# wo brought block by block, its first block on partitions 0 to 63 by eight transfers of eight partitions

## Chip, cores and metric

The kernel runs on one core of one Trainium2 chip. The metric is the device time of one execution in microseconds (us). Clock times below are us from the start of the profiled execution.

## The reference, cut to what matters

A decode step: attention for 4 tokens with 32 heads over an 8192-entry K and V cache (512 MB), the output projection with `wo` (4096 x 1024, 8 MB), and beside it a small MLP. The two results are mixed by a sigmoid gate.

```python
q = (x @ wq).reshape(B, Sq, H, Dh)
scores = einsum("bhqd,bhkd->bhqk", q, k_cache) * Dh ** -0.5
o = einsum("bhqk,bhkd->bhqd", softmax(scores), v_cache)
a = o.reshape(B, Sq, H * Dh) @ wo          # the part that the change touches
out = g * a + (1 - g) * b                  # b: the MLP branch
```

## The kernel before

K and V come in 64 pieces of 4 MB each, through a ring of five buffers. V lags K by four steps. At the end the projection multiplies the attention rows `LT` by `wo`, in eight blocks of 512 rows (1 MB, 8 KB on each of the 128 partitions, as the rows of the on-chip memory are called; 8 matmuls). The last group of heads must be finished (`flush`, `o_rows`) before the last two blocks can be used; blocks 0 to 5 need only what is known before the loop ends.

```python
ring = ctx.enter_context(tc.tile_pool(name="ring", bufs=5))
def slot():
    return ring.tile([P, RING], BF, name="piece", tag="piece")    # 128 x 32 KB
wov = A_wo.rearrange("(g p r) n -> p g r n", p=P, r=FR)           # FR = 4, 8 blocks g
# ... cut ...
def wo_piece(g0, g1, r0=0, r1=FR):
    ng, nr = g1 - g0, r1 - r0
    w = slot()[:, :ng * nr * D].rearrange("p (g r n) -> p g r n", g=ng, r=nr)
    nc.sync.dma_start(out=w.rearrange("p g r n -> p g (r n)"),
                      in_=wov[:, g0:g1, r0:r1].rearrange("p g r n -> p g (r n)"))
    def use():
        for g in range(ng):
            for r in range(nr):
                for n in range(NH):
                    mm_acc(acc[:, n * NB:(n + 1) * NB], LT[:, r0 + r, g0 + g, :], w[:, g, r, n * NB:(n + 1) * NB])
    return use
# ... cut ...
for u in range(NT + LAG):                 # NT = 64, LAG = 4
    if u < NT:
        k_piece(u)
    if u >= LAG:
        v_piece(u - LAG)                  # the last V piece comes in four transfers of 1 MB
    # ... cut: side work early in the loop ...
    if u == NT:
        o_rows(0, GE)                     # GE = 6: LT of blocks 0 to 5
        add_x()
GS = NWB // 2
last = [wo_piece(0, GS), wo_piece(GS, GE), wo_piece(GE, NWB - 1),
        wo_piece(NWB - 1, NWB, 0, FR - 1), wo_piece(NWB - 1, NWB, FR - 1, FR)]
flush()
o_rows(GE, NWB)
for use in last:
    use()
```

Of the kernel before, what the change touches and what calls it, by code (L numbers as in the profile page):

```python
# [9 lines left out]
BF = mybir.dt.bfloat16  # L10
F32 = mybir.dt.float32
# [8 lines left out]
def kernel(  # L20
# [22 lines left out]
    nc = tc.nc  # L43
    P = 128
    Bn, Sq, D = A_x.shape
# [11 lines left out]
    NT = Bn * H // HT  # L57
    LAG = 4
    FR = 4
    FG = F // (P * FR)  # L60
    NB = 512
    NH = D // NB
# [7 lines left out]
    const = ctx.enter_context(tc.tile_pool(name="const", bufs=1))  # L70
# [7 lines left out]
    ops = ctx.enter_context(tc.tile_pool(name="ops", bufs=2, space=PSUM))  # L78
    o2p = ctx.enter_context(tc.tile_pool(name="o2p", bufs=1, space=PSUM))

    def slot():
        return ring.tile([P, RING], BF, name="piece", tag="piece")
# [13 lines left out]
    identb = const.tile([P, P], BF)  # L96
# [37 lines left out]
    qa = const.tile([P, 4, H, Bn], BF)  # L134
    OT = const.tile([P, H, Bn], BF)
    LT = const.tile([P, FR, H // FR, Bn], BF)
    hT = const.tile([P, FG, FR, Bn], BF)
    sgb = const.tile([P, 2, Bn], F32)
    c12 = const.tile([P, 2, Bn], F32)
# [7 lines left out]
    acc = accp.tile([Bn, D], F32)  # L147

    def mm_acc(out_ap, lhsT, rhs, start=False):
        nc.tensor.matmul(out_ap, lhsT=lhsT, rhs=rhs, start=start, stop=True, skip_group_check=True)  # L150
# [15 lines left out]
    def add_x():  # L166
        xb = ptp.tile([Bn, D], BF, name="xb", bufs=1)
        nc.sync.dma_start(out=xb[:], in_=x2)
        xf = ptp.tile([Bn, D], F32, name="xf", bufs=1)
        nc.vector.tensor_copy(out=xf[:], in_=xb[:])  # L170
        for n in range(NH):
            mm_acc(acc[:, n * NB:(n + 1) * NB], dg[:], xf[:, n * NB:(n + 1) * NB])
# [50 lines left out]
    WB = P * FR // Dh  # L223
    NWB = H // WB

    def o_rows(g0, g1):

        n = g1 - g0
        lp = ops.tile([P, FR, n, Bn], F32, name="o_ps")
        for k in range(WB):  # L230
            for r in range(FR):
                nc.tensor.matmul(lp[32 * k:32 * k + 32, r], lhsT=identb[:, r:P:FR],
                                 rhs=OT[:, WB * g0 + k:WB * g1:WB, :], start=True, stop=True, skip_group_check=True)
        nc.vector.tensor_copy(out=LT[:, :, g0:g1, :], in_=lp[:])

    def wo_piece(g0, g1, r0=0, r1=FR):
        ng, nr = g1 - g0, r1 - r0
# [10 lines that stand above are left out]
# [6 lines left out]
    def flush():  # L254
        while pending:
            pending.pop(0)()
# [8 lines left out]
    def k_piece(u):  # L265
        b, h0 = heads(u)
        g, t = divmod(u, GT)
        Z = Zt[u % 2]
        for a in range(NQ):
            nc.gpsimd.tensor_copy(out=Z[32 * a:32 * a + 32, :, 31 + 32 * a:32 + 32 * a],  # L270
                                  in_=qa[32 * a:32 * a + 32, :, h0 + a // QH, b:b + 1])
        if t == 0:
            S_ps[g] = scp.tile([P, 512], F32, name="S_ps")
        sps = S_ps[g]
        kn = slot()
        nc.sync.dma_start(out=kn[:], in_=kv_view(A_k_cache, u))
        for c in range(JR // CJ):
            T = ttp.tile([P, CJ, 2, 32, 2], BF, name="T", tag="T")
            nc.vector.transpose(out=T[:].rearrange("p j h i e -> p (j h i e)").bitcast(U32),  # L279
                                in_=kn[:, c * CJ * Dh:(c + 1) * CJ * Dh].bitcast(U32))  # L280
            for jl in range(CJ // 16):
                jc = c * (CJ // 16) + jl
                s = 31 - (JC * t + jc)
                for he in range(4):
                    half, e = divmod(he, 2)
                    nc.tensor.matmul(sps[:, :], lhsT=Z[:, he, s:s + P], rhs=T[:, 16 * jl:16 * jl + 16, half, :, e],  # L286
                                     start=(t == 0 and jc == 0 and he == 0),
                                     stop=(t == GT - 1 and jc == JC - 1 and he == 3))
            if c == 0:
                flush()  # L290
        if t == GT - 1:
            softmax(g)
# [34 lines left out]
    def v_piece(u):  # L327
        b, h0 = heads(u)
        g, t = divmod(u, GT)
        B_ = PB[g % 2]  # L330
        vn = slot()
        vv = kv_view(A_v_cache, u)
        cut = 4 if u == NT - 1 else 1
        for c in range(cut):
            lo, hi = c * RING // cut, (c + 1) * RING // cut
            nc.sync.dma_start(out=vn[:, lo:hi], in_=vv[:, lo:hi])
        o_ps = ops.tile([P, 4 * Dh], F32, name="o_ps")
        n = 0
        for jc in range(JC):
            for uq in range(4):  # L340
                j0 = 16 * jc + 4 * uq
                nc.tensor.matmul(o_ps[32 * t:32 * t + NM, :], lhsT=B_[:, JC * t + jc, uq].rearrange("p s j -> p (s j)"),  # L342
                                 rhs=vn[:, j0 * Dh:(j0 + 4) * Dh], start=(n == 0), stop=(n == JR // 4 - 1))
                n += 1
                if n == 8:
                    flush()
        o_sb = OS[g % 2]
        nc.scalar.copy(out=o_sb[32 * t:32 * t + NM, :], in_=o_ps[32 * t:32 * t + NM, :])  # L348
        if t < GT - 1:
            return  # L350

        def finish():
            oT = o2p.tile([P, GH], F32, name="oT")
            for q in range(4):
                nc.tensor.matmul(oT[:, :], lhsT=o_sb[:, q * Dh:(q + 1) * Dh],  # L355
                                 rhs=selg[:, q].rearrange("p t s -> p (t s)"), start=(q == 0), stop=(q == 3))
            hg = h0 + HT - GH
            nc.vector.scalar_tensor_tensor(out=OT[:, hg:hg + GH, b], in0=oT[:, :], scalar=sgb[:, 1, b:b + 1],  # L358
                                           in1=rinv_t.pop(g)[:], op0=ALU.mult, op1=ALU.mult)
        pending.append(finish)  # L360
# [8 lines left out]
    GE = NWB - GH // WB  # L369
    for u in range(NT + LAG):  # L370
# [3 lines that stand above are left out]
            v_piece(u - LAG)  # L374
        if side:
            side.pop(0)()
        if u == NT:
            o_rows(0, GE)
            add_x()
    GS = NWB // 2  # L380
    last = [wo_piece(0, GS), wo_piece(GS, GE), wo_piece(GE, NWB - 1),
            wo_piece(NWB - 1, NWB, 0, FR - 1), wo_piece(NWB - 1, NWB, FR - 1, FR)]
    flush()
    o_rows(GE, NWB)
    for use in last:
        use()
# [35 lines left out]
```

## Time and profile before

| | before |
|---|---|
| median time (4 runs beside the change) | 1355.85 us |
| span of the profiled execution | 1354.6 us |
| last V piece landed | 1325.4 us |
| first wo transfer (4 MB) landed | 1335.38 us |
| last wo transfer landed | 1345.35 us |
| last matmul ended | 1351.7 us |

Two lines of the page: the busy share of the 16 DMA engines in 40 slices of the span, in tenths, and the DMA queue that carries the data (packets, MB, share of 16 engines' span).

```profile
DMA  9999999999999999999999999999999999999996
q1 hardware_dynamic: 21904, 575.69, 99.0%
```

So the kernel is a stream of bytes until its last 20 us or so. The end of the chain of waits (start, duration, what) shows what those are. PE is TensorE, `o_ps` the attention weights times V, `acc` the sum of the projection.

```profile
1287.47 7.01 PE o_ps L342 x32
...
1295.99 39.39 DMA piece<-in_A_wo_dram
1335.38 0.04 issue
1335.42 16.27 PE acc L150 x64
1351.69 0.02 issue
1351.71 0.57 ACT res L390
```

The 39.39 us are one wo transfer from issue to landing: it stands in line behind V, whose last landing is at 1325.4. After it come all 64 matmuls of the projection in one go. The first transfer holds four blocks, so nothing can start before all 4 MB are there. The same in stretches (from:to, length, busy time and count on PE, PE's weight loads, VectorE, ScalarE and GpSimd, then granted TensorE clock, DMA share, GB/s):

```profile
1315.00:1318.00 3.00, 3.00 (x17) 1.22 (x15) 0.00 (x0) 0.58 (x1) 0.00 (x0) 1.00 1.00 418
...
1330.00:1340.00 10.00, 5.51 (x33) 2.21 (x33) 0.43 (x2) 0.00 (x0) 0.00 (x0) 0.66 0.92 381
1340.00:1346.00 6.00, 6.00 (x29) 2.39 (x28) 0.00 (x0) 0.00 (x0) 0.00 (x0) 0.99 0.41 165
1346.00:1355.00 9.00, 5.68 (x27) 2.04 (x24) 0.68 (x1) 0.57 (x1) 0.00 (x0) 0.93 0.00 1
```

TensorE is half idle while the last bytes come (1330 to 1340, at a clock of 0.66: the clock records put it at half from 1333.25 to 1340.07, beginning in an idle stretch of 4.16 us), and busy for 5.68 us when no byte is left to come. The DMA share falls to 0.41 in 1340 to 1346. The reason is in the landings. In the trace a piece of V raises its completion semaphore, the counter that tells of its landing, 16 times, which I read as once for each of the 16 engines. For the wo transfer of 0.75 MB these times, read from the trace's semaphore events, are:

```
1336.63 1336.76 1336.98 1337.96 1338.01 1339.47 1339.65 | 1343.22 | 1344.25 1344.26 1344.28 1344.36 1344.36 1344.60 1344.63 1344.71
```

Seven engines are ahead of the other nine, by 3.6 us and more (1339.65 against 1343.22).

### The profile page before, as it was taken

The page shows a single profiled execution, that of the slowest core. Times are in us where ns is not written, and L with a number is a line of the kernel's source. Part 1 is how long each engine was busy: PE and PEld are TensorE (multiplying, and loading weights), DVE is VectorE, ACT ScalarE, POOL GpSimd, SP SyncE. Part 2 cuts the span into 40 slices and gives each one's busy share as a digit, 9 for nine tenths or more (in the row PEclk, how much of TensorE's full clock was granted, in tenths as well). Part 3 has the DMA queues.
Part 4 walks back from the last instruction along what each step waited for, and adds up shares of the span by engine and source line. Part 5 has one row for each costly group of instructions (what it writes and reads, how often), then busy time and mean ns, then how long its engine had stood idle before and what let it go on. Part 6 is the DMA issues. An engine that isn't in the chain of part 4 may idle for free.

```text
span 1354.6 us, 11809 instructions
## 1 busy us (share of the span) xinstructions
PE 1065.1 (79%) x5112; PEld 434.5 (32%) x5112; DVE 622.3 (46%) x403; ACT 71.0 (5%) x118; POOL 86.8 (6%) x326
## 2 busy tenths in 40 slices
PE   2775888888687878879787777868877787888797
PEld 2432333333233323333233333323333332333333
DVE  1553345544543554455355534545454445445500
ACT  0000000000000000000000000000000000000010
POOL 2000000000000000000000000000000000000000
PEclk9877998889899988989999898989989888998898
DMA  9999999999999999999999999999999999999996
GB/s 403 429 431 430 425 430 432 432 432 431 429 432 430 433 430 431 427 431 432 431 433 432 433 428 432 430 428 433 431 433 430 432 428 430 432 431 433 432 419 258
DMA packets 21976, 576.46 MB, mean 426 GB/s; under 512 B 2322, under 2 KB 2330, under 8 KB 2596
## 3 DMA queue, kind: packets, MB, share of 16 engines
q1 hardware_dynamic: 21904, 575.69, 99.0%
q8 instruction: 40, 0.66, 0.2%
q14 instruction: 12, 0.10, 0.0%
q10 hardware_dynamic: 20, 0.02, 0.0%
HBM read 575.69 MB, written 0.01 MB: 425 GB/s over the span
## 4 chain that ended last, share of the span: by engine, by line
DMA 47%; PE 31%; DVE 12%; issue 7%; POOL 2%; ACT 1%; DVEq 0%; SPq 0%; ACTq 0%
DMA piece<-in_A_k_cache_dram 45%; PE o_ps L342 16%; PE S_ps L286 12%; DVE T L279 10%; DMA piece<-in_A_wo_dram 3%; PE acc L150 2%; PE oT L355 1%; DVE PT L311 1%; PE shr L150 1%; POOL PB_142 L316 1%; POOL PB_143 L316 1%; POOL tot L320 0%; ACT OS_138 L348 0%; ACT OS_139 L348 0%; DVE OT L358 0%
## 5 line engine op out<-in xcount | busy, mean ns | idle before, releaser
L279 DVE STREAM_TRANSPOSE T<-piece 128x2048 uint32<-128x2048 uint32 x256 | 576.1, 2288 | 474.7 <-DMA piece<-in_A_k_cache_dram 370.0
L286 PE MATMUL S_ps<-T,Z_140 128*128 128x512 bf16 x1024 | 287.9, 436 | 164.9 <-DVE T L279 164.6
L286 PE MATMUL S_ps<-T,Z_141 128*128 128x512 bf16 x1024 | 259.1, 401 | 84.1 <-DVE T L279 83.8
L342 PE MATMUL o_ps<-piece,PB_143 128*8 128x512 bf16 x1024 | 226.5, 381 | 2.1 <-POOL PB_143 L316 2.1
L342 PE MATMUL o_ps<-piece,PB_142 128*8 128x512 bf16 x1024 | 226.2, 379 | 0.0
L286 PEld LDWEIGHTS <-Z_140 128*128 128x128 bf16 x1024 | 111.3, 109 | 337.2 <-issue 256.4
L286 PEld LDWEIGHTS <-Z_141 128*128 128x128 bf16 x1024 | 102.1, 101 | 239.8 <-issue 143.6
L342 PEld LDWEIGHTS <-PB_143 128*8 128x8 bf16 x1024 | 86.5, 87 | 139.9 <-issue 15.3
L342 PEld LDWEIGHTS <-PB_142 128*8 128x8 bf16 x1024 | 86.4, 87 | 137.3 <-issue 13.6
L358 DVE SCALAR_TENSOR_TENSOR OT<-oT,sgb,rinv 128x8 bf16<-128x8 f32 x16 | 3.8, 236 | 126.0 <-PE oT L355 126.0
L270 POOL COPY Z_141<-qa 32x4 bf16<-32x4 bf16 x128 | 25.1, 196 | 525.1 <-PE S_ps L286 519.5
L270 POOL COPY Z_140<-qa 32x4 bf16<-32x4 bf16 x128 | 25.1, 196 | 496.4 <-PE S_ps L286 482.5
L348 ACT COPY OS_138<-o_ps 8x512 f32<-8x512 f32 x32 | 18.5, 577 | 594.2 <-PE o_ps L342 594.2
L348 ACT COPY OS_139<-o_ps 8x512 f32<-8x512 f32 x32 | 18.5, 577 | 536.8 <-PE o_ps L342 536.8
L150 PE MATMUL shr<-xw,piece 128*128 128x4 bf16 x704 | 22.6, 170 | 2.8 <-DMA piece<-in_A_wq_dram 2.6
L150 PEld LDWEIGHTS <-piece 128*128 128x128 bf16 x704 | 22.6, 113 | 3.9 <-DMA piece<-in_A_wq_dram 2.7
L150 PE MATMUL acc<-piece,LT 128*4 128x512 bf16 x64 | 16.3, 421 | 4.2 <-DMA piece<-in_A_wo_dram 4.2
L322 DVE RECIPROCAL rinv<-tot 128x8 f32<-128x8 f32 x16 | 3.2, 203 | 25.6 <-POOL tot L320 25.6
L355 PE MATMUL oT<-selg,OS_139 128*128 128x8 f32 x64 | 8.5, 259 | 5.7 <-ACT OS_139 L348 5.7
L355 PE MATMUL oT<-selg,OS_138 128*128 128x8 f32 x64 | 8.5, 259 | 5.7 <-ACT OS_138 L348 5.7
L316 POOL COPY PB_143<-PT 64x512 bf16<-64x512 bf16 x8 | 8.3, 1032 | 65.9 <-DVE rex L318 65.9
L150 PE MATMUL acc<-piece,hT 128*4 128x512 bf16 x56 | 12.4, 379 | 0.0
(99 smaller groups left out, 145.9 us busy)
## 6 DMA issues: line engine op xcount, KB each, us to landing
piece<-in_A_k_cache_dram SPq DMA_DIRECT2D x64, 4096.0 KB, 39.7
piece<-in_A_v_cache_dram SPq DMA_DIRECT2D x63, 4096.0 KB, 38.7
piece<-in_A_wq_dram SPq DMA_DIRECT2D x2, 4096.0 KB, 13.5
piece<-in_B_w_gate_dram SPq DMA_DIRECT2D x2, 3584.0 KB, 39.9
piece<-in_B_w_up_dram SPq DMA_DIRECT2D x2, 3584.0 KB
piece<-in_B_w_down_dram SPq DMA_DIRECT2D x1, 4096.0 KB, 39.9
piece<-in_A_v_cache_dram SPq DMA_DIRECT2D x4, 1024.0 KB, 38.4
piece<-in_A_wo_dram SPq DMA_DIRECT2D x1, 4096.0 KB, 39.4
```

The lines of the kernel that those rows point to most:

```text
L150: nc.tensor.matmul(out_ap, lhsT=lhsT, rhs=rhs, start=start, stop=True, skip_group_check=True)
L270: nc.gpsimd.tensor_copy(out=Z[32 * a:32 * a + 32, :, 31 + 32 * a:32 + 32 * a], in_=qa[32 * a:32 * a + 32, :, h0 + a // QH, b:b + 1])
L279: nc.vector.transpose(out=T[:].rearrange("p j h i e -> p (j h i e)").bitcast(U32), in_=kn[:, c * CJ * Dh:(c + 1) * CJ * Dh].bitcast(U32))
L286: nc.tensor.matmul(sps[:, :], lhsT=Z[:, he, s:s + P], rhs=T[:, 16 * jl:16 * jl + 16, half, :, e], start=(t == 0 and jc == 0 and he == 0), ...
L311: nc.vector.transpose(out=PT[:].rearrange("p j i -> p (j i)"), in_=PTs[:])
L316: nc.gpsimd.tensor_copy(out=B_[W:P, :, :, 1, :], in_=Pv[W:P])
L322: nc.vector.reciprocal(out=rinv[:], in_=tot[:])
L342: nc.tensor.matmul(o_ps[32 * t:32 * t + NM, :], lhsT=B_[:, JC * t + jc, uq].rearrange("p s j -> p (s j)"), rhs=vn[:, j0 * Dh:(j0 + 4) * Dh ...
L348: nc.scalar.copy(out=o_sb[32 * t:32 * t + NM, :], in_=o_ps[32 * t:32 * t + NM, :])
L355: nc.tensor.matmul(oT[:, :], lhsT=o_sb[:, q * Dh:(q + 1) * Dh], rhs=selg[:, q].rearrange("p t s -> p (t s)"), start=(q == 0), stop=(q == 3))
L358: nc.vector.scalar_tensor_tensor(out=OT[:, hg:hg + GH, b], in0=oT[:, :], scalar=sgb[:, 1, b:b + 1], in1=rinv_t.pop(g)[:], op0=ALU.mult, op ...
```

## The change

It does two things. wo now comes in transfers of one block, so that its matmuls can follow the bytes. And block 0 is laid on partitions 0 to 63 alone, two segments of 8 KB on each, by eight transfers of eight partitions. The intent, as I read it: these go to the engines that are ahead and take half a megabyte off the others. Blocks 0 and 1 also move ahead of the last V piece. The core of the diff:

```diff
+    def half_rows(g):
+        lp = ops.tile([P // 2, 2, FR, Bn], F32, name="o_ps")
+        for k in range(WB):
+            for r in range(FR):
+                k2 = k % 2
+                nc.tensor.matmul(lp[32 * k2:32 * k2 + 32, k // 2, r], lhsT=identb[:, r:P:FR], rhs=OT[:, WB * g + k, :],
+                                 start=True, stop=True, skip_group_check=True)
+        nc.vector.tensor_copy(out=LTh[:], in_=lp[:])
+
+    def wo_half(g):
+        w = slot()[0:P // 2, :2 * FR * D].rearrange("p (s r n) -> p s r n", s=2, r=FR)
+        wv = A_wo[512 * g:512 * (g + 1)].rearrange("(s p r) n -> p s (r n)", s=2, r=FR)
+        for p0 in (0, 32):
+            for i in range(4):
+                sl = slice(p0 + i, p0 + 32, 4)
+                nc.sync.dma_start(out=w[sl].rearrange("p s r n -> p s (r n)"), in_=wv[sl])
+        for s in range(2):
+            for r in range(FR):
+                for n in range(NH):
+                    mm_acc(acc[:, n * NB:(n + 1) * NB], LTh[:, s, r, :], w[:, s, r, n * NB:(n + 1) * NB])
@@ in the loop
         if u == NT:
-            o_rows(0, GE)
+            half_rows(0)
+            o_rows(1, GE)
             add_x()
+        if u == NT + LAG - 2:
+            wo_half(0)
+            wo_piece(1, 2)()
-    GS = NWB // 2
-    last = [wo_piece(0, GS), wo_piece(GS, GE), wo_piece(GE, NWB - 1),
-            wo_piece(NWB - 1, NWB, 0, FR - 1), wo_piece(NWB - 1, NWB, FR - 1, FR)]
+    last = [wo_piece(g, g + 1) for g in range(2, NWB - 1)]
+    last += [wo_piece(NWB - 1, NWB, 0, FR - 1), wo_piece(NWB - 1, NWB, FR - 1, FR)]
```

More of the change, by code (lines that the diff above doesn't have):

```diff
@@ L136 @@
     LT = const.tile([P, FR, H // FR, Bn], BF)
+    LTh = const.tile([P // 2, 2, FR, Bn], BF)
     hT = const.tile([P, FG, FR, Bn], BF)
```

## The prediction

> **What bounds the kernel.** The DMA engines, until the last 19 us. The page's slices show DMA at 9 in 39 of 40; q1's packets take 99.0% of 16 engines' span. The chain of waits ends with 39.39 us of waiting for wo, then 16.27 us of 64 matmuls (1335.42 to 1351.7), then 2.9 us to the end at 1354.6. The matmuls wait for the first wo transfer (4 MB, four blocks or nothing, landed at 1335.38), although the last transfer lands at 1345.35: 6.4 us of the tail is TensorE behind the last byte. Eleven of the 64 matmuls take 427 ns, the others near 210: the granted clock is 0.66 in 1330 to 1340.
>
> **Imbalance.** The 16 landings of one transfer are spread: in the last one seven engines land 1337.3 to 1340.3, nine 1343.9 to 1345.35. [...] The four-row x transfer indeed lands four times, on three early engines and a late one. [...] The intent: 0.5 MB more on the early half.
>
> **Costs and savings.** A 1 MB block costs every engine 2.48 us (quarters of the last V). [...] But there is a new wait: SP rotates eight completion semaphores; the eighth half transfer waits for V piece 62's landing (1315.65), and behind it stand wo block 1 and V 63, queued at 1286 before. [...] packets end near 1315.0, landing 1315.65, two issues of 0.35, about 0.8 from issue to packet (as the output transfer shows): 1.9 us lost. [...] last landing 1346.3 to 1347.4, 1 to 2 us later than before.
>
> TensorE: 24 matmuls (block 0 doubled to 16 on 64 rows, block 1) move before V 63, 5.0 us; V 63 ends near 1334.3 instead of 1328.85; the finish chain (2.7 us, as before) gives LT at 1337.0; 48 more matmuls: 10.1 us [...]. TensorE ends at 1347 to 1350.5, against 1351.7. All of this is critical. Net: about -3 us.
>
> **Prediction: 1352.8 us, 1350.3 to 1355.3 in 8 of 10. Faster by over 2%: 0.01; within 2%: 0.98; slower: 0.01.**
>
> **What would show it.** 24 wo matmuls before V 63's, 48 after 1336; eight half transfers with eight engine landings each, the eighth issued just after V 62 landed; a DMA dip near 1316; last wo landing at 1346 to 1347.5; no 39 us wait for wo; last PE at 1347 to 1350.5.
>
> **What would make it wrong.** Half transfers spread over 16 engines: no extra load, about 1.5 us earlier. A wider bubble: some us slower. The engines' drift settling otherwise, [...]: up to 2 us faster. Slot waits of the last blocks (each needs one consumed): DMA gaps after 1335.

The marked cuts take out what no trace of this case shows: which numbered engines serve which transfer, and what makes TensorE's clock fall. With them go terms of the sum, all of them my estimates. I had assumed that the half block goes to eight engines, one of them late: 2.48 us more on that one and 2.48 less on the other eight engines, against the 1.9 us lost. And I had allowed 1.7 to 3.4 us for a slow clock in the finish gap, half of the 3.41 and 6.83 us that single stretches at half clock last in the clock records of the kernel before. The sum came to a last wo landing of 1346.3 to 1347.4 and, from 1337.0 us with the 10.1 us and the clock's share, to a last matmul at 1347 to 1350.5, against 1351.7: about 3 us less.

## The result

| | before | changed |
|---|---|---|
| median time (4 runs each) | 1355.85 us | 1353.67 us |
| lowest to highest | 1355.29 to 1356.14 | 1353.16 to 1354.22 |
| span of the profiled execution | 1354.6 us | 1351.4 us |
| last wo landing | 1345.35 us | 1347.24 us |
| last matmul ended | 1351.7 us | 1348.55 us |

The ratio is 0.9985 with a 95% interval of 0.9967 to 1.0002: the same within 2%, and in this first comparison not clear of 1 (in e5, the same kernel but for its ring buffers, it is: 0.9985, 0.9973 to 0.9998).

The page's slices and queue line:

```profile
DMA  9999999999999999999999999999999999999988
q1 hardware_dynamic: 22016, 575.69, 99.3%
```

The end of the chain of waits:

```profile
1318.24 14.07 DMA piece<-in_A_v_cache_dram
1332.31 0.04 issue
1332.36 1.90 PE o_ps L366 x8
1334.26 0.02 issue
1334.27 10.47 DMA piece<-in_A_wo_dram
1344.74 0.04 issue
1344.79 3.77 PE acc L151 x16
1348.55 0.02 issue
1348.58 0.57 ACT res L417
```

The wait of 39 us for one wo transfer is gone. It ends with 16 matmuls behind the landing of block 6, not with 64. The same stretches (columns as before):

```profile
1315.00:1318.00 3.00, 3.00 (x19) 1.28 (x18) 0.00 (x0) 0.58 (x1) 0.00 (x0) 1.00 0.50 137
1318.00:1330.00 12.00, 12.00 (x60) 4.54 (x59) 0.00 (x0) 0.58 (x1) 0.00 (x0) 1.00 1.00 421
1330.00:1340.00 10.00, 8.75 (x59) 4.05 (x58) 0.42 (x2) 0.58 (x1) 0.00 (x0) 1.00 1.01 421
1340.00:1346.00 6.00, 4.91 (x23) 1.78 (x22) 0.00 (x0) 0.00 (x0) 0.00 (x0) 1.00 0.90 371
```

TensorE now works while the bytes come, at full clock. But at 1315 to 1318 the DMA share is 0.50, where it was 1.00. What happened there is in the instructions of SyncE, which issues the transfers: first its timeline (start, duration, what, count), then the line of its waits (who waited for what: us in total, times, longest).

```profile
1285.58 30.47 SPq L254 DMA_DIRECT2D piece<-in_A_wo_dram  x8
1316.16 0.37 SPq L263 DMA_DIRECT2D piece<-in_A_wo_dram  x1
1316.63 2.06 SPq L360 DMA_DIRECT2D piece<-in_A_v_cache_dram  x4
```

```profile
SPq L254 <- DMA piece<-in_A_v_cache_dram: 24.7, 3, 9.0
```

The built program rotates eight completion semaphores for these transfers: in the trace V piece 62 raises number 103, and the half transfers 104, 107, 108, 109, 110, 100, 102 and again 103. The eighth waits for 103, that is for the one just before them all, V piece 62: it was issued at 1315.37, V 62 having landed at 1315.36. Block 1 and the last V piece stand behind it and are issued at 1316.16 and later. Before, the last V piece was issued at 1285.5, far ahead of its turn. Engines with packets in flight, counted in the trace:

| at | 1314.0 | 1315.0 | 1316.0 | 1317.0 | 1317.5 |
|---|---|---|---|---|---|
| before | 16 | 16 | 16 or more | 16 | 16 or more |
| changed | 8 | 3 | 3 | 6 | 16 |

A count over 16 is rounding at a change of packet. The three that stay busy have half transfers to do. Landings of V 62 and of the first half transfer in the changed kernel:

```
V 62:       1307.07 1307.48 1307.54 1308.69 1308.75 1308.90 1309.87 | 1313.50 1313.69 | 1314.91 1314.93 1314.95 1314.96 1315.15 1315.27 1315.36
first half: 1307.69 1309.30 1309.37 1309.51 1310.49 | 1314.31 | 1315.51 1315.53
```

Of the eight engines with the half transfers, five are early, one in between and two as late as any. Those two do block 0's double share (eight times two packets of 0.309 us, about 0.62 us each time) on top of being late. At the landing of block 1 they are alone behind the rest: fourteen engines at 1320.80 to 1321.29, two at 1322.35 and 1322.37. At the final wo transfer thirteen land at 1345.68 to 1346.17 and three at 1347.19 to 1347.24. The third is late from the landing at 1342.2 on; it is probably the engine that had a 16 KB packet of instructions (1.09 us) at 1338.7, but the trace does not number the engines.

### The profile page after: what moved, and what is told of

It reads as the page before. It is cut to its first block, busy times and chain, and to the rows that moved or that the text cites. A ratio compares the mean times of both kernels' runs of the same rounds, so it can differ in the third digit from the quotient of the medians.

```text
span 1351.4 us, 11876 instructions
## 1 busy us (share of the span) xinstructions
PE 1068.6 (79%) x5136; PEld 435.7 (32%) x5136; DVE 623.1 (46%) x404; ACT 70.9 (5%) x118; POOL 86.1 (6%) x326
## 4 chain that ended last, share of the span: by engine, by line
DMA 46%; PE 35%; DVE 12%; issue 4%; POOL 2%; ACT 1%; SPq 0%; DVEq 0%; ACTq 0%
DMA piece<-in_A_k_cache_dram 44%; PE o_ps L366 17%; PE S_ps L310 15%; DVE T L303 11%; PE oT L379 1%; DMA piece<-in_A_v_cache_dram 1%; PE acc L151 1%; DMA piece<-in_A_wo_dram 1%; DVE PT L335 1%; POOL PB_143 L340 1%; POOL PB_142 L340 1%; PE shr L151 1%; POOL tot L344 0%; ACT OS_138 L372 0%; ACT OS_139 L372 0%
## 5 line engine op out<-in xcount | busy, mean ns | idle before, releaser
L151 PE MATMUL acc<-piece,LT 128*4 128x512 bf16 x56 | 12.9, 378 | 1.1 <-DMA piece<-in_A_wo_dram 1.1
```

The lines of the kernel that those rows point to most:

```text
L151: nc.tensor.matmul(out_ap, lhsT=lhsT, rhs=rhs, start=start, stop=True, skip_group_check=True)
```

## The experiments

Each run was timed in five rounds beside the kernel before, except the last two. All eight ran on the same chip, the first four and the next four together; medians of the kernel before were 1356.15 and 1356.02 us (the second takes in the nine runs of the first and one more). The last two ran on another chip. All gave correct results.

| run | median us | ratio to before (95%) | last wo landing | last matmul end | span |
|---|---|---|---|---|---|
| e1_split_only | 1351.20 | 0.9965 (0.9953 to 0.9978) | 1345.17 | 1346.47 | 1349.4 |
| e2_full_block_early | 1351.26 | 0.9965 (0.9952 to 0.9977) | 1345.11 | 1346.42 | 1349.4 |
| e3_half_by_16_rows | 1358.36 | 1.0017 (1.0004 to 1.0031) | 1351.95 | 1353.88 | 1356.9 |
| e4_half_alone | 1356.58 | 1.0005 (0.9992 to 1.0018) | 1347.28 | 1351.95 | 1354.9 |
| e5_half_shared_slots | 1353.61 | 0.9985 (0.9973 to 0.9998) | 1347.13 | 1348.46 | 1351.4 |
| e6_half_interleaved | 1357.95 | 1.0015 (1.0001 to 1.0029) | 1347.18 | 1350.05 | 1353.0 |
| e7_half_on_64_to_127 | 1359.30 | 1.0025 (1.0011 to 1.0039) | 1352.97 | 1354.29 | 1357.2 |
| e8_blocks_no_half | 1351.10 | 0.9964 (0.9951 to 0.9978) | 1345.04 | 1346.46 | 1349.5 |

### e1_split_only: the split alone

```diff
 (against the kernel before)
-    last = [wo_piece(0, GS), wo_piece(GS, GE), wo_piece(GE, NWB - 1), ...
+    last = [wo_piece(g, g + 1) for g in range(NWB - 1)]
+    last += [wo_piece(NWB - 1, NWB, 0, FR - 1), wo_piece(NWB - 1, NWB, FR - 1, FR)]
```

> The kernel before with wo in 1 MB transfers alone: all eight blocks on 128 partitions, after the last V piece, no half block. Theory (the split is the gain, the half block a loss): last wo landing stays at about 1345.4 us, the last matmul follows it by under 1 us instead of 6.4, time about 1350.2 us, that is 5.6 below before and 3 or more below the change. Rival 1 (the half block is the gain): 1354.5 us or more. Rival 2 (fine pieces run into ring-slot waits): gaps in the DMA share after 1330 and a last landing after 1347.

Measured: 4.95 us below before (1356.15 to 1351.20), 5.6 expected. The last landing stays (1345.17 against 1345.35) and the last matmul follows it by 1.30 us instead of 6.4; under 1 was expected. The end of its chain of waits:

```profile
1329.26 1.07 PE oT L355 x8
...
1330.98 15.49 PE acc L150 x63
1346.47 0.02 issue
```

TensorE starts on wo at 1330.9 instead of 1335.4 and is then never without work. The clock records put 1331.81 to 1335.22 at half clock, so TensorE, and not the last byte, ended this tail. Of the 5.2 us by which the last matmul ended earlier, about 4.5 are the earlier start; by my estimate the rest is clock, since eleven matmuls at half clock before and about eight here lose 2.3 and 1.7 us. The split is worth more than the whole change. Neither rival held: some engines had gaps (9 to 12 of 16 busy at 1333 to 1334.5, while block 5 waited for a ring buffer until 1333.38), but the late ones always had work, and they set the last landing.

### e2_full_block_early: block 0 whole, in the same place

```diff
 (against the changed kernel)
-            half_rows(0)
-            o_rows(1, GE)
+            o_rows(0, GE)
-            wo_half(0)
+            wo_piece(0, 1)()
             wo_piece(1, 2)()
```

> The changed kernel with block 0 as one transfer over 128 partitions in the same place. Theory: nothing waits for the landing of V piece 62, DMA share stays at 1.0 at 1310 to 1318, last wo landing 1345.4 against 1347.2 in the change, time 1350.5 to 1351.5. Rival (putting the block on the early engines helps): later than the change, 1354 or more.

Measured: 1351.26 us, within the expected range. All 16 engines are busy without a break from 1300 to 1331, and the last landing is at 1345.11. The end of its chain has the shape of the change's, about 2.1 us sooner:

```profile
1332.27 10.34 DMA piece<-in_A_wo_dram
1342.62 0.04 issue
1342.66 3.76 PE acc L151 x16
1346.42 0.02 issue
```

This differs from the change only in how block 0 lies and comes (and so in 8 matmuls on it instead of 16). The half block therefore costs 0.9985 against 0.9965 of before, about 2.7 us (2.4 by the medians; e5 against e8, timed together, differ by 2.5, though e8 also cuts block 7 finer), of which 2.1 us are its later last landing. Whether blocks 0 and 1 come before or after the last V piece (e2 or e1) makes no difference.

### e3_half_by_16_rows: the same half block in four transfers

```diff
 (against the changed kernel)
-            for i in range(4):
-                sl = slice(p0 + i, p0 + 32, 4)
+            for i in range(2):
+                sl = slice(p0 + i, p0 + 32, 2)
```

> The changed kernel with the same half block on partitions 0 to 63, brought by four transfers of sixteen partitions. Theory (how many engines a transfer gets follows from its row count): sixteen landings for each of the four, no engine is loaded more, no dip near 1316, last wo landing about 1345.4, time about 1351.2. Rival (what counts is that the block lies on half of the partitions): last landing 1347 or later and time as the change, about 1353.7.

Measured: 1358.36 us, and my expectation was wrong by 7 us. The first half of it was right: each of these transfers landed sixteen times, where the eight-row ones of the change landed eight times. But the landings of one engine's successive transfers are about 1.25 us apart, where the two packets of 8 KB took 0.62 in the change. Stretches of its profile:

```profile
1307.00:1310.00 3.00, 3.00 (x25) 0.74 (x25) 0.42 (x2) 0.39 (x1) 0.00 (x0) 1.00 1.08 243
...
1316.00:1319.00 3.00, 0.15 (x1) 0.00 (x0) 0.00 (x0) 0.58 (x1) 0.00 (x0) 0.86 0.92 183
1319.00:1322.00 3.00, 1.65 (x4) 0.48 (x5) 0.00 (x0) 0.00 (x0) 0.00 (x0) 0.50 0.98 208
```

The engines are busy (DMA share 0.92 to 1.08) but move about half of the usual 430 GB/s. In 1316 to 1319 an 8 KB packet took 0.645 us in the median instead of 0.309, and one of 32 KB of V piece 62 took 2.48 instead of 1.21. V 62 landed at 1320.31, and TensorE sat idle at 1316 to 1319 for want of it. The half block, 1 MB, came in four steps of about 1.25 us, near 210 GB/s; e2, with block 0 over all 128 partitions, had no such stretch (1351.26 us). The rival was thus right that the half of the partitions counts, and with its last landing (1347 or later; 1351.95 came), though not with its time. But half of the partitions alone does not do it: in the changed kernel, where eight rows four partitions apart make one transfer, the same packets on the same partitions took 0.309 us. That would be a reason for the odd form of the change. Why the packets slow down in one form and not in the other is not shown.

### e4_half_alone: the half block without the split

```diff
 (against the changed kernel)
             wo_half(0)
-            wo_piece(1, 2)()
-    last = [wo_piece(g, g + 1) for g in range(2, NWB - 1)]
+    last = [wo_piece(1, GS), wo_piece(GS, GE), wo_piece(GE, NWB - 1), ...
```

> The half block in its place, block 1 back in the tail and the tail in big transfers as before (3, 2, 1, 0.75, 0.25 MB). Theory: last wo landing 1347.2 as in the change, the tail's 56 matmuls start when the 3 MB transfer lands at about 1337.3, end near 1351.3; time 1354.5 to 1356.5, no gain over before. Rival (the half block is what gains): 1353.7 or less.

Measured: 1356.58 us against 1356.15 before, no gain, 0.1 above the expected range. The last landing is at 1347.28 and the tail's matmuls start at 1338.4, with their end at 1351.95. The 3 MB transfer had landed at 1337.38, as expected; the finish of the last heads released the tail. The half block brings nothing of its own, and what the change gained is the split.

### e5_half_shared_slots and e6_half_interleaved: the idle stretch or the double load?

Both were seen in the changed trace. e5 is the control: blocks 2 to 5 share one ring buffer and blocks 6 and 7 another. e6 then moves half transfers 5 to 8 between the quarters of the last V piece.

```diff
 (e5: against the changed kernel)
-    last = [wo_piece(g, g + 1) for g in range(2, NWB - 1)]
-    last += [wo_piece(NWB - 1, NWB, 0, FR - 1), wo_piece(NWB - 1, NWB, FR - 1, FR)]
+    last = wo_slot([(g, 0, FR) for g in range(2, GE)])
+    last += wo_slot([(GE, 0, FR), (NWB - 1, 0, FR - 1), (NWB - 1, FR - 1, FR)])
 (e6: against e5, in wo_half)
+        for i in range(4):
+            bring(0, i)
+        later.extend(lambda i=i: bring(32, i) for i in range(4))
 (e6: in v_piece, behind each of the four transfers of the last piece)
+            if later and cut == 4:
+                later.pop(0)()
 (e6: at the end)
+    use_half()
     flush()
```

> The changed kernel with blocks 2 to 5 in one ring buffer and blocks 6 and 7 in another (same transfers, no waits for a free buffer): the control for the next run. Both theories: same as the change, about 1353.5 us; three engines busy at 1315 to 1316.5; two engines' last landing near 1347.2, the other fourteen by 1346.2.

> The same, but half transfers 5 to 8 are issued between the quarters of V piece 63, so that 2 MB for all engines are queued when V piece 62 lands; the half block's matmuls move behind V 63's. Both the idle stretch and the load on two late engines were read from the change's trace; this run takes away the first alone. Theory (the doubly loaded late engines set the last byte): all 16 engines busy at 1315 to 1317, fourteen engines' last landing near 1343.7, two still at 1347.2; TensorE ends near 1349.3, time 1353.5 to 1355. Rival (the idle stretch set the last byte): last landing 1345.4 or earlier on all engines.

e5 came out as the change in every point that is compared here: 1353.61 us, three engines busy at 1315 to 1316.5, thirteen engines' last landing by 1345.85 and three at 1346.96 to 1347.13, as in the change.

e6 took most of the idle stretch away: 11 to 14 engines are busy at 1315 to 1316.3 and 15 or more from 1316.5, where the change had three until 1316.8. Thirteen engines then had their last landing by 1342.53 (sooner than I had expected), one at 1345.07 and the last two at 1346.95 and 1347.18. So the last byte did not move, although most engines were done 3 us sooner. Landings of the last wo transfer:

```
change: 1345.68 1345.69 1345.69 1345.70 1345.75 1345.76 1345.80 1345.82 1345.95 1345.96 1346.03 1346.16 1346.17 | 1347.19 1347.22 1347.24
e6:     1340.88 1341.70 1341.73 1341.75 1341.76 1342.05 1342.06 1342.12 1342.15 1342.39 1342.45 1342.52 1342.53 | 1345.07 | 1346.95 1347.18
```

The load on two late engines sets it, as the theory said; filling the idle stretch alone does not bring it forward. The theory missed the time: 1357.95 in the median, with 1354.67 to 1359.8 (the half block's matmuls stand in the tail here, and the tail waits on TensorE). The scatter was looked into with the last two runs.

### e7_half_on_64_to_127: the half block on the upper partitions

```diff
 (against the changed kernel)
-        w = slot()[0:P // 2, :2 * FR * D].rearrange(...)
+        w = slot()[P // 2:P, :2 * FR * D].rearrange(...)
 (and the rows of LTh on partitions 64 to 127)
```

> The changed kernel with the half block on partitions 64 to 127. Theory [...]: five of the eight landings of the first half transfer by 1311, as in the change, and the packets [...] take up to 0.6 us for 8 KB and up to 2.4 us for 32 KB instead of 0.31 and 1.21; V 62 lands later than 1315.4, time 1354 to 1358. Rival (the engines follow the partitions): at most two landings of the first half transfer by 1311, packets keep 0.31 us[...].

The theory is that eight rows go to the same eight engines whatever their partitions.

Landings of the first half transfer: 1308.16, 1309.47, 1310.00, 1310.45, 1312.65, then 1318.45, 1320.16, 1320.27. Five are still well ahead of the other three; four instead of five were in by 1311. With the rival there would have been two at most, since seven engines run ahead and five of them are among the eight of the change. So here the eight-row transfers went to the same eight engines on either half of the partitions, as far as landing times can tell without engine numbers. In 1310 to 1313 the packets took 0.635 us for 8 KB and 2.45 for 32 KB (medians), as expected, and V 62 landed at 1320.88. Why they slow down on these partitions, and in the change on the others not, is not shown. The time, 1359.3, is above the expected range: a delay of 5.5 us of V 62 passes whole to the end (5.6 us over the change).

### e8_blocks_no_half: a candidate for the best version

```diff
 (against e2)
+            for use in wo_slot([(0, 0, FR), (1, 0, FR)]):
+                use()
+    last = wo_slot([(g, 0, FR) for g in range(2, GE)])
+    last += wo_slot([(GE, 0, FR)] + [(NWB - 1, r, r + 1) for r in range(FR)])
```

> Candidate for the best version: no half block, blocks 0 and 1 early on 128 partitions in one ring buffer, blocks 2 to 5 in one, 6 and 7 in one, block 7 in four transfers of 0.25 MB. Theory: last landing 1345.1 as in e2_full_block_early, TensorE's last matmul 0.6 us behind it instead of 1.3; time 1350.5 us, 0.7 below e2 and e1, hardly apart from them by time alone. Rival (smaller transfers cost as much as they save): 1351.2 or more.

Measured: 1351.10 us, as e1 and e2. The expected 0.7 us did not show. The bytes were as planned (1345.04), but TensorE ran its 48 tail matmuls from 1334.4 to 1346.46 without a wait, part of it at half clock:

```profile
1336.00:1338.00 2.00, 2.00 (x6) 0.63 (x5) 0.00 (x0) 0.00 (x0) 0.00 (x0) 0.50 0.92 367
1338.00:1340.00 2.00, 2.00 (x10) 0.70 (x9) 0.00 (x0) 0.00 (x0) 0.00 (x0) 0.93 0.64 258
```

Six matmuls in 2 us at clock 0.50, ten at 0.93. The clock records put 3.41 us at half clock, from 1334.87. The waits for landings in e2's tail (0.37 and 0.58 us) are gone, and a slow clock took their place.

### e9_interleaved_again and e10_interleaved_third: the scatter of e6

The same kernel as e6, one look each.

> The interleaved half block once more, for the scatter of its times (1354.67 to 1359.8): a profile of one of the longer executions, if one is caught. If the longer ones come from the half block's transfers, packets of 8 KB over 0.31 us or engines without work show between 1315 and 1335; if from elsewhere, these stay as in the first look. No time is predicted but the range of the first five.

> As e9_interleaved_again, a third look at the same kernel, for the same purpose.

They took 1358.00 and 1360.03 us, so two of the longer executions were caught. The last landings are 1347.15 and 1347.48, against 1347.18 in the short one, and the 8 KB packets of 1315 to 1335 took 0.309 us in the median in all three (over 0.34: 26 of some 1000 in the short one, 11 and 25 in the long ones): the half block's transfers are not the cause. One stretch of e6, of e9 and of e10, in this order:

```profile
1336.00:1346.00 10.00, 10.00 (x51) 3.76 (x48) 0.19 (x1) 0.00 (x0) 0.00 (x0) 1.00 0.63 259
```

```profile
1336.00:1346.00 10.00, 10.00 (x35) 3.08 (x32) 0.19 (x1) 0.00 (x0) 0.00 (x0) 0.66 0.63 259
```

```profile
1336.00:1346.00 10.00, 9.98 (x40) 2.99 (x40) 0.19 (x1) 0.00 (x0) 0.00 (x0) 0.54 0.64 262
```

The bytes are alike (0.63 to 0.64, 259 to 262 GB/s); the clock is 1.00, 0.66 and 0.54. In the chain of waits the same 64 matmuls took 14.01, 17.34 and 19.02 us. The clock at half lasted 6.83 and 10.24 us in e9 and e10 and 3.41 in e1 and e8, and one kernel (e6, e9 and e10) shows three outcomes behind the same finish chain. In the 15 us before each of these falls TensorE's longest idle stretch was 0.7 us (e1, e8) to 1.2 us (e9, e10), and e6, whose clock stayed full in this stretch, had one of 1.2 us too. What brings the clock down is not shown here. A tail that waits on TensorE can scatter so (e6: 1354.67 to 1359.8 us); the five runs of e1 (1351.14 to 1351.40) and the four of e8 (1350.95 to 1351.48), whose tails wait on it too, did not.

## Why the prediction was right

It forecast 1352.8 us (1350.3 to 1355.3), within 2%; 1353.67 was measured.

- **The 64 matmuls behind one 4 MB transfer: right.** TensorE's lag behind the last landing fell from 6.4 to 1.3 us. e1 shows that this, alone, is worth 4.95 us.
- **The completion semaphores: right, undersized.** The eighth half transfer was issued 0.01 us after V 62 landed. I took 0.35 us for the issue of each transfer; an eight-row one took 0.68. The idle engines resumed only between 1316.8 and 1317.5, and eleven of their first 8 KB packets took 0.79 to 1.15 us instead of 0.31, which the sum did not have. I had put the loss at 1.9 us; it was about 3.6, since thirteen engines had their last landing by 1346.17 here and by 1342.53 where the stretch was filled (e6). They came out later than before (1345.35), where I had those without half transfers end near 1344.2.
- **Who carries the half block: right in kind, wrong in number.** That the half block goes to eight engines, seven of them early and one late, was my assumption, and the step that failed. Eight engines do serve each half transfer (eight landings each, in e7 too), but five of them are early, one is in between and two are late. I had only the four landings of one small transfer to go by (1289.22, 1290.23, 1291.18 and 1294.75 for x in the kernel before). The last landing came as forecast all the same (1347.24; 1346.3 to 1347.4): one doubly loaded late engine was in the sum, and a second one beside it adds nothing to the wait for the last. That was luck. e6 confirmed that these engines set it.
- **The clock in the finish gap: wrong here.** I held a fall for likely, which was an assumption. The profiled execution of the change kept 1.00 through 1330 to 1346. In e1 and e8 the clock was at half for 3.41 us, in e9 and e10 for 6.83 and 10.24; in e4 the tail's 55 matmuls took 13.52 us, 0.246 each, against 0.219 in e6 at full clock (64 in 14.01).
- **The end: right, in part by luck.** The last matmul ended at 1348.55 (forecast 1347 to 1350.5), and TensorE did its 24 early wo matmuls before the last V piece was done. But with the clock full, the sum (1337.0 and 10.1 us) gives 1347.1. The rest of the way is two waits for the landings of blocks 5 and 6 (0.49 and 0.60 us), which the sum did not have; they stood in for the clock fall that did not come.

The gain of about 2 us is thus a gain of about 5 from the split, less some 2.5 to 2.7 for the half block, whose aim of easing the late engines failed: two late engines were among those that it loads. A better version than both kernels is the split without the half block: e1 is the simplest, at 1351.20 us.

What stays open: why seven engines run ahead, which of the 16 the two late ones are (the traces number no engine), what makes the clock fall in one execution and not in another, and how the median of the change would move with its own clock scatter, which was not looked at.

## What to carry to other kernels

Split the last loads so that the work on them can follow the bytes, and measure the split alone before anything clever is added to it. Before you shift load between DMA engines, list the landing times of a transfer that uses just those engines: the average of a group hides its latest member, and the latest one is what is waited for. Count transfers as well as bytes: here eight small ones used up the eight completion semaphores, and the large ones behind them were issued 30 us later than before.
